# Squared-ReLU attention and a capacity-routed expert layer on one core: one z piece per go, goes of four in the whole first group, and the three engines' order fixed from the first step

## The chip, the core and the metric

The kernel runs on one core of one Trainium2 chip. The core's engines work side by side, each through its own list of instructions in order: TensorE (PE in the rows; its weight loads are PEld), VectorE (DVE), ScalarE (ACT), GpSimd (POOL) and SyncE (SP, which here issues the plain DMAs). An engine that reaches an instruction whose operands are not ready stands still, and so does everything behind it in its list. The metric is the device time of one execution in microseconds.

## The reference, cut to what matters

```python
# u, v: (8, 2496, 256); z: (8, 2496, 64)
scores = (1 / 2496) * np.matmul(z, z.transpose(0, 2, 1))
attn = np.maximum(scores, 0.0) ** 2
out = u * np.matmul(attn, v)                     # (8, 2496, 256)
x = out.reshape(19968, 256)                      # then the expert layer
logits = x @ w_gate                              # 8 experts, 2496 tokens each at most
# tokens go to experts greedily, in falling order of logit; y = relu(x @ w1[e]) @ w2[e]
```

Everything is float32. The change is in the attention part alone.

## The kernel before

**Numbers as two parts.** A float32 value is kept as a high part that TensorE takes directly and a low part, value minus high part. A product is made of three passes: high by high, high by low, low by high. So z is held as `zh` and `zl`, v as `vh` and `vl`, and the squared scores as `hi` and `lo`.

**Steps.** Attention runs over 800 steps (b, g, kt): 8 batches, 5 groups of 512 queries (the last of 448), 20 key tiles of 128 (the last of 64). A batch is 100 steps, a group 20. Loop index n drives everything; `LA = 4`, `GO = 10`, `KT = 20`.
- `scores` makes a "go" of steps at once on TensorE: for each pair of key tiles three passes of two 64-row matmuls (line 863) into two of the six PSUM buffers `sc`. A go is named here by the n at which it stands: go n makes the scores of steps n+4 and on. Before the change the goes have 4, 4, 4 and 2 steps, then ten each.
- `rectify` empties an `sc` buffer into an `r` tile, on ScalarE (line 875); the second of each go of ten is done on VectorE (line 873).
- `square` (ScalarE, line 879), `split_hi` (ScalarE line 884, or for three in ten VectorE line 886) and `split_lo` (VectorE, line 895) follow for step n+4, one step per n.
- `av(n)` multiplies with v on TensorE: six matmuls of 512 columns per step (lines 908, 910, 911) into `acc`.
- `split_v` makes `vh` on ScalarE (844) and `vl` on VectorE (845); in the first batch one key tile per step.
- After a group, `take_acc`, `turn_back`, `post_mul` and the gate logits (line 959, VectorE, 32 per group spread over later steps) finish its rows.

**z pieces.** The transposed z of a batch, tiles `zh` and `zl`, is made in five pieces, one for each four key tiles. `load_z` brings a piece in by DMA (`zin`, two buffers). `z_turn` transposes it on TensorE (two matmuls, line 807) into an `sc` buffer. For batches 1 to 7 `z_whole` copies that to `zsh` (ScalarE, line 814) and subtracts to `zsl` (VectorE, line 815), one buffer each, and eight DMAs (line 821) put the two tiles into `zh` and `zl`. For the first batch `z_parts` writes the pieces into place by engine (lines 830, 831) and `swap_z` copies the other halves by DMA. In `at(m, z_turn, b, g)` the number m is the step: before the change batch b, with first step n0 = 100 b, turns its pieces at n0-59, n0-55, n0-49, n0-46 and n0-43, which is two in go n0-60 and three in go n0-50.

**What sets the order.** From n = 10 to the last steps TensorE, ScalarE and VectorE run in the order in which the code is written (`tc.manual_schedule`, lines 1070 to 1072). Ahead of that, and on SP throughout, a scheduler that works with estimated costs places the instructions.

Of the kernel before, what the change touches and what calls it, by code (L numbers as in the profile page):

```python
# [21 lines left out]
def tile_attention_then_moe(ctx, tc, u, v, z, w_gate, w1, w2, out):  # L22
# [40 lines left out]
    nc.vector.tensor_scalar(first["at0"], at0_f, 4096.0, -32768.0, op0=OP.mult, op1=OP.add)  # L63

    attention(tc, u, v, z, w_gate, xd, identf, made, first, 1.0 / S)
    moe(tc, xd, first, jp, identf, w1, w2, out, B, S, consts)

# [638 lines left out]
def attention(tc, u, v, z, w_gate, xd, identf, made, first, scale):  # L706
    nc = tc.nc
    B, S, D = u.shape
    DQ = z.shape[-1]
    lg, m = first["lg"], first["m"]  # L710
# [3 lines left out]
    KT = NT + 1  # L714
    DH = D // 128
    NQ = KT // 4
    J = B * NT + B // 2
    JP = lg.shape[1]
    LA = 4
    RING = KT + 2  # L720
    SCB = 6
    GO = KT // 2
    with ExitStack() as ctx:
# [99 lines left out]
        def z_parts(b, g):  # L823
            c = slice(512 * g, 512 * g + 512)
            p = ZT.pop((b, g))
            zh, zl = [t[b][:, c].rearrange("p (i s q) -> p i s q", s=2, q=128) for t in (ZH, ZL)]
            src = p[:, :256].rearrange("p (i q) -> p i q", q=128)
            for s in range(2):
                r = slice(DQ * s, DQ * s + DQ)
                nc.scalar.activation(zh[r, :, s], src[r], AF.Copy)  # L830
                nc.vector.tensor_sub(zl[r, :, s], src[r], zh[r, :, s].bitcast(F32))

        def swap_z(b, c):
# [16 lines left out]
        def width(g):  # L850
            return min(512, S - 512 * g)

        def scores(lo, hi):
            for n in range(lo, hi, 2):
                b, g, kt = seq[n]
                w = width(g)
                q = slice(g * 512, g * 512 + w)
                pair = [ps.tile([128, 512], F32, name="sc", bufs=SCB)[:, :w] for _ in range(2)]
                for key, query in ((ZH, ZH), (ZH, ZL), (ZL, ZH)):
                    for s in range(2):  # L860
                        r = slice(DQ * s, DQ * s + DQ)
                        k = (kt + s) * 128
                        nc.tensor.matmul(pair[s], key[b][r, k:k + 128], query[b][r, q],  # L863
                                         start=key is ZH and query is ZH, stop=key is ZL)
                for s in range(2):
                    SC[n + s] = pair[s]
                    rectify(n + s, n + s == lo + 1 and hi - lo == GO)

        def rectify(n, aside):
            p = SC.pop(n)  # L870
            r = wk.tile([128, 512], F32, name="r", bufs=GO + 3)[:, :p.shape[1]]
            if aside:
                nc.vector.tensor_scalar(r, p, 0.0, scale, op0=OP.max, op1=OP.mult)
            else:
                recent["r"] = nc.scalar.activation(r, p, AF.Relu, scale=scale)  # L875
            R[n] = r

        def square(n):
            nc.scalar.activation(R[n], R[n], AF.Square)  # L879

        def split_hi(n):
            h = wk.tile([128, 512], F32R, name="hi", bufs=LA + 1)[:, :width(seq[n][1])]
            if (n - LA) % GO not in (0, 4, 8):
                nc.scalar.activation(h, R[n], AF.Copy)  # L884
            else:
                nc.vector.tensor_copy(h, R[n])
            HI[n] = h

        def split_lo(n):
            a, h = R.pop(n), HI[n]  # L890
            if seq[n][2] == NT:
                nc.vector.tensor_sub(h[TL:], a[TL:], h[TL:].bitcast(F32))
                return
            l = wk.tile([128, 512], F32R, name="lo", bufs=LA + 1)[:, :width(seq[n][1])]
            recent["l"] = nc.vector.tensor_sub(l, a, h.bitcast(F32))  # L895
            LO[n] = l

        def av(n):
            b, g, kt = seq[n]
            if kt == 0:  # L900
                ACC[b, g] = [ps.tile([128, 512], F32, name=f"acc{d}", bufs=1) for d in range(2)]
            last = kt == NT
            h, l = HI.pop(n), LO.pop(n, None)
            for d in range(2):
                o = ACC[b, g][d][:, :width(g)]
                c = slice(d * 128, (d + 1) * 128)
                vh, vl = VH[b, kt][:, c], VL[b, kt][:, c]
                nc.tensor.matmul(o, vh, h, start=(kt == 0), stop=False)  # L908
                if not last:
                    nc.tensor.matmul(o, vh, l, start=False, stop=False)  # L910
                nc.tensor.matmul(o, vl, h, start=False, stop=last)  # L911
# [84 lines left out]
        def at(n, f, *a):  # L996
            todo.setdefault(n, []).append((f, a))

        def logits_at(m0):
            if m0 + KT < B * NQ * KT:  # L1000
                mid, end = {NQ - 3: (18, 14), NQ - 2: (10, 14)}.get(m0 // KT % NQ - 1, (14, 14))
                return [m0 + GO] * mid + [m0 + KT] * end + [m0 + KT + 4 + i for i in range(4 * E - mid - end)]
            return [m0 + GO] * 16 + [m0 + GO + 1 + i // 3 for i in range(16)]
# [7 lines left out]
        for b in range(B):  # L1011
            for g in range(NQ):
                n0 = (b * NQ + g) * KT
                m0 = n0 + KT
                t = m0 + (0 if m0 == B * NQ * KT else 2)
                for d in range(2):
                    at(m0 - 1, take_acc, b, g, d)
                at(t, turn_back, b, g)
                for d in range(2):
                    at(t + 1, post_mul, b, g, d)  # L1020
                for e, n in enumerate(logits_at(m0) if m0 < B * NQ * KT else ()):
                    first_in.setdefault(n, []).append((post_logits, (b, g, e // E, e % E)))
                if b or g:
                    at(n0 - 3, load_u, b, g)
            n0 = b * NQ * KT
            if b == B - 1:
                at(B * NQ * KT + 2, last_logits, b, NQ - 1)
                at(B * NQ * KT + 3, settle, b * NT + 4 * (NQ - 1), (b + 1) * NT)
                at(B * NQ * KT + 3, settle, B * NT, J)
            if b:  # L1030
                for g in range(NQ):
                    m = n0 - 3 * KT + (4 * g + 1 if 4 * g + 2 < GO else KT - 3 * (NQ - g))
                    at(m - 5, load_z, b, g)
                    at(m, z_turn, b, g)
                    at(m + 1, z_whole, b, g)
                    at(n0 - KT + 4 * g - 8, load_v, b, g)
                for kt in range(KT):
                    at(n0 - KT + kt, split_v, b, kt)
            else:
                for kt in range(KT):  # L1040
                    at(kt - 4, split_v, 0, kt)
                for g in range(1, NQ):
                    t = min(4 * g - LA, GO) - 1
                    at(t, z_turn, 0, g)
                    at(t, z_parts, 0, g)
                    at(t + 1, swap_z, 0, slice(512 * g, 512 * g + 512))
                    if g >= 3:
                        at(4 * g - 13, load_z, 0, g)
                        at(4 * g - 11, load_v, 0, g)
# [11 lines left out]
        at(13, load_gate)  # L1061
        at(18, gate_rows)
        N = len(seq)
        begins = [0, LA, 2 * LA, 3 * LA] + list(range(LA + GO, N, GO))
        goes = {lo - LA: (lo, hi) for lo, hi in zip(begins, begins[1:] + [N])}
        fixed = ExitStack()
        for n in range(-LA, N + 4 * E):
            if n == 2:
                early.close()
            if n == GO:  # L1070
                fixed.enter_context(tc.manual_schedule(
                    engines={mybir.EngineType.PE, mybir.EngineType.Activation, mybir.EngineType.DVE}))
            if n == N - 4:
                fixed.close()
            if n in goes:
                scores(*goes[n])
            for f, a in first_in.pop(n, []):
                f(*a)
            m = n + LA
            if 0 <= m < N:  # L1080
                square(m)
                split_hi(m)
                split_lo(m)
            for k in sorted(k for k in todo if k < n):
                for f, a in todo.pop(k):
                    f(*a)
            if 0 <= n < N:
                av(n)
            for f, a in todo.pop(n, []):
                f(*a)  # L1090
# [25 lines left out]
```

## Time and profile before

| what | us |
|---|---|
| median of 3 runs | 2606.8 (2606.2 to 2617.64) |
| the profiled execution: its time | 2609.21 |
| its span, first to last instruction | 2607.4 |
| PE busy / DVE busy / ACT busy | 2522.9 / 2016.1 / 1543.1 |
| PE busy from 120.1 to 161.3 (41.2 long) | 37.3 |
| PE busy from 1393.3 to 1428.9 (35.6 long) | 35.6 |

The span is the profiler's view of one execution; 1.8 us lie around it. A busy time counts what an engine spent in instructions, so 2607.4 less 2522.9 is the time in which TensorE had nothing running. The last two rows are the same kind of stretch, three goes and a bit in the second batch (with z pieces for the next one) and two goes in the last batch (which has no next one).

### The profile page before, as it was taken

What the parts mean: (1) busy time and instruction counts of PE and PEld (TensorE: products, weight loads), DVE (VectorE), ACT (ScalarE), POOL (GpSimd) and SP (SyncE); (2) the same over time, 40 slices, a digit from 0 to 9 for tenths busy, and PEclk for the clock granted to TensorE, in tenths of its full rate; (3) what the DMA queues carried; (4) which work ended last, traced back from release to release, by engine and by line L of the source; (5) the groups of instructions that cost most, each with busy time, mean ns of one, the idle gap of its engine ahead of it and who ended that gap; (6) DMA issues with size and microseconds to landing.
All of it is one profiled execution on the core that took longest, in us unless ns stands there. A gap on an engine that the chain in (4) does not pass through costs nothing.

```text
span 2607.4 us, 44969 instructions
## 1 busy us (share of the span) xinstructions
PE 2522.9 (97%) x16328; PEld 2137.9 (82%) x16328; DVE 2016.1 (77%) x6105; ACT 1543.1 (59%) x2901; POOL 358.7 (14%) x507
## 2 busy tenths in 40 slices
PE   8999999999999999999999989999999999999998
PEld 5778787788788788787878768888989898989997
DVE  5788788888798898888888878869686968696322
ACT  7878788787788788787888412323333333333332
POOL 2000000000000000000000003233333333334321
PEclk9999999999999999999999989999999999999999
DMA  4121221210221221212100011112121212121110
GB/s 138 55 70 51 72 66 48 78 63 32 83 72 33 67 72 58 75 57 62 51 32 25 16 42 46 62 46 74 40 73 40 74 40 72 41 90 56 47 42 24
DMA packets 93599, 148.82 MB, mean 57 GB/s; under 512 B 16192, under 2 KB 61632, under 8 KB 93376
## 3 DMA queue, kind: packets, MB, share of 16 engines
q1 hardware_dynamic: 78272, 105.03, 13.0%
q0 software_dynamic: 15104, 40.91, 5.0%
q8 instruction: 128, 2.10, 0.3%
q14 instruction: 95, 0.78, 0.1%
HBM read 85.60 MB, written 40.89 MB: 49 GB/s over the span
## 4 chain that ended last, share of the span: by engine, by line
PE 82%; DVE 10%; ACT 3%; DMA 2%; issue 1%; SPq 1%; POOL 0%; POOLq 0%; DVEq 0%; ACTq 0%
PE acc L908 13%; PE acc L911 12%; PE acc L910 12%; PE sc L863 10%; PE y L602 5%; PE hp L571 5%; PE y L604 5%; PE y L603 5%; PE hp L572 5%; PE hp L573 5%; PE srch L243 2%; PE sc L931 1%; PE xp L555 1%; ACT r L879 1%; DMA zl<-zsl 1%
## 5 line engine op out<-in xcount | busy, mean ns | idle before, releaser
L908 PE MATMUL acc<-hi,vh 128*128 128x512 f32 (+1 forms) x1600 | 633.6, 396 | 4.2 <-ACT vh L844 3.7
L911 PE MATMUL acc<-hi,vl 128*128 128x512 f32 (+1 forms) x1600 | 617.7, 386 | 0.0
L895 DVE TENSOR_TENSOR lo<-r,hi 128x512 fp32r<-128x512 f32 (+1 forms) x760 | 504.2, 677 | 115.2 <-ACT hi L884 105.6
L910 PE MATMUL acc<-lo,vh 128*128 128x512 f32 (+1 forms) x1520 | 587.4, 387 | 0.4 <-DVE lo L895 0.2
L590 ACT ACTIVATE hh<-hp 128x512 fp32r<-128x512 f32 (+1 forms) x320 | 187.6, 586 | 548.4 <-PE hp L573 470.3
L879 ACT ACTIVATE r<-r 128x512 f32<-128x512 f32 (+1 forms) x800 | 474.1, 621 | 0.2
L959 DVE SCALAR_TENSOR_TENSOR lt<-xs,wgb 128x256 bf16<-128x256 f32 x1248 | 447.8, 421 | 0.5
L884 ACT ACTIVATE hi<-r 128x512 fp32r<-128x512 f32 (+1 forms) x560 | 348.3, 622 | 140.2 <-issue 83.9
L875 ACT ACTIVATE r<-sc 128x512 f32<-128x512 f32 (+1 forms) x722 | 364.2, 611 | 90.7 <-PE sc L863 84.8
L908 PEld LDWEIGHTS acc<-hi,vh 128*128 128x128 f32 x1600 | 301.6, 189 | 85.2 <-issue 28.6
L602 PE MATMUL y<-w2h,hh 128*128 128x256 f32 (+1 forms) x1280 | 366.9, 287 | 1.2 <-ACT y L629 1.2
L603 PE MATMUL y<-w2l,hh 128*128 128x256 f32 (+1 forms) x1280 | 363.0, 284 | 0.0
L911 PEld LDWEIGHTS acc<-hi,vl 128*128 128x128 f32 x1600 | 301.3, 188 | 58.0 <-issue 1.3
L910 PEld LDWEIGHTS acc<-lo,vh 128*128 128x128 f32 x1520 | 287.0, 189 | 49.8 <-DVE lo L895 1.8
L571 PE MATMUL hp<-xh,w1h 128*128 128x512 f32 (+2 forms) x646 | 262.7, 408 | 0.7 <-ACT xh L564 0.7
L572 PE MATMUL hp<-xl,w1h 128*128 128x512 f32 (+2 forms) x646 | 251.2, 389 | 0.0
L602 PEld LDWEIGHTS y<-w2h,hh 128*128 128x128 f32 (+1 forms) x1280 | 241.2, 188 | 11.8 <-ACT y L629 1.6
L573 PE MATMUL hp<-xh,w1l 128*128 128x512 f32 (+2 forms) x646 | 249.8, 387 | 0.0
L603 PEld LDWEIGHTS y<-w2l,hh 128*128 128x128 f32 (+1 forms) x1280 | 241.0, 188 | 8.8
L635 POOL DMA_INDIRECT out_dram<-y,idx x160 | 176.7, 1105 | 385.3 <-ACT y L629 337.5
L863 PE MATMUL sc<-zh 64*128 64x512 f32 (+1 forms) x800 | 192.7, 424 | 26.6 <-DVE zsl L815 11.8
L496 POOL DMA_INDIRECT xg<-xd,idx x160 | 162.9, 1018 | 389.3 <-PE xp L555 133.1
(1159 smaller groups left out, 3721.8 us busy)
## 6 DMA issues: line engine op xcount, KB each, us to landing
vr<-in_v_dram SPq DMA_DIRECT2D x32, 512.0 KB, 3.7
ur<-in_u_dram SPq DMA_DIRECT2D x32, 512.0 KB, 4.3
xd<-xs SPq DMA_DIRECT2D x32, 512.0 KB, 2.9
wr<-in_moe_w_dram SPq DMA_DIRECT2D x32, 512.0 KB, 5.3
zh<-zsh SPq DMA_DIRECT2D x140, 64.0 KB, 2.1
zl<-zsl SPq DMA_DIRECT2D x140, 64.0 KB, 2.0
zin<-in_z_dram SPq DMA_DIRECT2D x31, 128.0 KB, 2.2
vr<-in_v_dram SPq DMA_DIRECT2D x8, 384.0 KB, 3.3
```

The lines of the kernel that those rows point to most:

```text
L571: nc.tensor.matmul(p[:, c], wh, xh, start=(d == 0), stop=False)
L572: nc.tensor.matmul(p[:, c], wh, xl, start=False, stop=False)
L573: nc.tensor.matmul(p[:, c], wl, xh, start=False, stop=(d == DH - 1))
L602: nc.tensor.matmul(o, h[:, c], wh, start=first, stop=False, skip_group_check=True)
L603: nc.tensor.matmul(o, h[:, c], wl, start=False, stop=False, skip_group_check=True)
L863: nc.tensor.matmul(pair[s], key[b][r, k:k + 128], query[b][r, q], start=key is ZH and query is ZH, stop=key is ZL)
L879: nc.scalar.activation(R[n], R[n], AF.Square)
L895: recent["l"] = nc.vector.tensor_sub(l, a, h.bitcast(F32))
L908: nc.tensor.matmul(o, vh, h, start=(kt == 0), stop=False)
L910: nc.tensor.matmul(o, vh, l, start=False, stop=False)
L911: nc.tensor.matmul(o, vl, h, start=False, stop=last)
L959: nc.vector.scalar_tensor_tensor(t[r], XS[b, g][r, i], 1.0, WG["rows"][r, e], op0=OP.mult, op1=OP.mult, accum_out=lg[r, j, e:e + 1])
```

## The change

- Batches 1 to 7 turn one z piece per go, five steps after its start: m = n0 + 10 (g - 8) + 5, so n0-75, -65, -55, -45, -35; `load_z` stands nine steps ahead instead of five.
- The first group is made in goes of four to its end: 4, 4, 4, 4, 4, 4, then ten each. From step 24 on goes begin where they did.
- In a go of any length (so in the last one of six too) the second rectification is on VectorE.
- In the first group all high parts are made on VectorE.
- In the first batch the turn of piece g, its parts and its swap stand at steps 4g-7, 4g-6 and 4g-5, and both ScalarE parts stand ahead of both VectorE parts.
- The written order holds on the three engines from n = -4, the first step.

```diff
             for s in range(2):
                 r = slice(DQ * s, DQ * s + DQ)
                 nc.scalar.activation(zh[r, :, s], src[r], AF.Copy)
+            for s in range(2):
+                r = slice(DQ * s, DQ * s + DQ)
                 nc.vector.tensor_sub(zl[r, :, s], src[r], zh[r, :, s].bitcast(F32))
...
-                    rectify(n + s, n + s == lo + 1 and hi - lo == GO)
+                    rectify(n + s, n + s == lo + 1)
...
-            if (n - LA) % GO not in (0, 4, 8):
+            if n >= KT and (n - LA) % GO not in (0, 4, 8):
                 nc.scalar.activation(h, R[n], AF.Copy)
             else:
                 nc.vector.tensor_copy(h, R[n])
...
-                    m = n0 - 3 * KT + (4 * g + 1 if 4 * g + 2 < GO else KT - 3 * (NQ - g))
-                    at(m - 5, load_z, b, g)
+                    m = n0 + GO * (g - 2 * NQ + 2) + 5
+                    at(m - 9, load_z, b, g)
                     at(m, z_turn, b, g)
                     at(m + 1, z_whole, b, g)
...
-                    t = min(4 * g - LA, GO) - 1
+                    t = 4 * g - LA - 3
                     at(t, z_turn, 0, g)
-                    at(t, z_parts, 0, g)
-                    at(t + 1, swap_z, 0, slice(512 * g, 512 * g + 512))
+                    at(t + 1, z_parts, 0, g)
+                    at(t + 2, swap_z, 0, slice(512 * g, 512 * g + 512))
...
-        begins = [0, LA, 2 * LA, 3 * LA] + list(range(LA + GO, N, GO))
+        begins = list(range(0, KT + LA, LA)) + list(range(KT + LA, N, GO))
...
-            if n == GO:
+            if n == -LA:
                 fixed.enter_context(tc.manual_schedule(
                     engines={mybir.EngineType.PE, mybir.EngineType.Activation, mybir.EngineType.DVE}))
```

ScalarE in the first batch, go n = 50, before: the pieces of batch 1 pass through `zsh` (`at0` closes the group; `hi` and `r` belong to steps 55 to 63).

```order
L884 ACTIVATE hi_1433<-r_1339 128x512
L814 ACTIVATE zsh_1443<-sc_1429 128x256
L879 ACTIVATE r_1341<-r_1341 128x512
L884 ACTIVATE hi_1460<-r_1341 128x512
L879 ACTIVATE r_1351<-r_1351 128x512
L879 ACTIVATE r_1353<-r_1353 128x512
L884 ACTIVATE hi_1485<-r_1353 128x512
L814 ACTIVATE zsh_1494<-sc_1481 128x256
L879 ACTIVATE r_1363<-r_1363 128x512
L884 ACTIVATE hi_1507<-r_1363 128x512
L814 ACTIVATE zsh_1544<-sc_1530 128x256
L919 ACTIVATE at0_1565<-acc0_1152 128x512
```

The same engine and go in the changed kernel, where line numbers are two higher from there on: one piece is left in this go.

```order
L886 ACTIVATE hi_1478<-r_1368 128x512
L881 ACTIVATE r_1378<-r_1378 128x512
L886 ACTIVATE hi_1491<-r_1378 128x512
L814 ACTIVATE zsh_1501<-sc_1487 128x256
L881 ACTIVATE r_1380<-r_1380 128x512
L886 ACTIVATE hi_1518<-r_1380 128x512
L881 ACTIVATE r_1390<-r_1390 128x512
L881 ACTIVATE r_1392<-r_1392 128x512
L886 ACTIVATE hi_1542<-r_1392 128x512
L921 ACTIVATE at0_1550<-acc0_1188 128x512
```

The other two pieces of the three stand in goes n = 40 and n = 60 now.

VectorE at the start of the program, before: steps 0 to 3 and the first batch's z piece 1 (`zl_126<-sc_194`), as the scheduler placed them.

```order
L895 TENSOR_TENSOR lo_161<-r_142,hi_159 128x512
L845 TENSOR_TENSOR vl_164<-vr_113,vh_163 128x256
L895 TENSOR_TENSOR lo_170<-r_144,hi_168 128x512
L845 TENSOR_TENSOR vl_173<-vr_113,vh_172 128x256
L886 CAST hi_177<-r_154 128x512
L895 TENSOR_TENSOR lo_179<-r_154,hi_177 128x512
L845 TENSOR_TENSOR vl_182<-vr_113,vh_181 128x256
L895 TENSOR_TENSOR lo_188<-r_156,hi_186 128x512
L845 TENSOR_TENSOR vl_191<-vr_113,vh_190 128x256
L831 TENSOR_TENSOR zl_126<-sc_194,zh_125 64x2x128 x2
```

The same place in the changed kernel: a rectification (line 875) comes first, every step has its `hi` here, and the z piece stands between the third and the fourth step.

```order
L875 TENSOR_SCALAR r_146<-sc_137 128x512
L888 CAST hi_161<-r_144 128x512
L897 TENSOR_TENSOR lo_163<-r_144,hi_161 128x512
L847 TENSOR_TENSOR vl_166<-vr_113,vh_165 128x256
L888 CAST hi_170<-r_146 128x512
L897 TENSOR_TENSOR lo_172<-r_146,hi_170 128x512
L847 TENSOR_TENSOR vl_175<-vr_113,vh_174 128x256
L888 CAST hi_182<-r_156 128x512
L897 TENSOR_TENSOR lo_184<-r_156,hi_182 128x512
L847 TENSOR_TENSOR vl_187<-vr_113,vh_186 128x256
L833 TENSOR_TENSOR zl_126<-sc_178,zh_125 64x2x128 x2
L888 CAST hi_195<-r_158 128x512
```

TensorE where the second go of scores is made, before: the scheduler took `av` of steps 0 to 2 first, and put matmuls of step 2 and 3 (`acc`) in between the scores (`sc`).

```order
L910 MATMUL acc1_233<-lo_179,vh_181 128x512
L863 MATMUL sc_203<-zh_125 128x512
L863 MATMUL sc_203<-zl_126,zh_125 128x512
L911 MATMUL acc0_232<-hi_177,vl_182 128x512
L911 MATMUL acc1_233<-hi_177,vl_182 128x512
L908 MATMUL acc0_232<-hi_186,vh_190 128x512
L910 MATMUL acc0_232<-lo_188,vh_190 128x512
L863 MATMUL sc_203<-zh_125,zl_126 128x512
L863 MATMUL sc_204<-zh_125 128x512
L863 MATMUL sc_204<-zl_126,zh_125 128x512
L863 MATMUL sc_215<-zh_125 128x512
```

In the changed kernel the second go (`sc_209` to `sc_222`) stands right behind the turn of z piece 1 (`sc_178`), whole, and ahead of the first `acc`.

```order
L807 MATMUL sc_178<-identf_63,zin_115 128x128 x2
L865 MATMUL sc_209<-zh_125 128x512
L865 MATMUL sc_210<-zh_125 128x512
L865 MATMUL sc_209<-zl_126,zh_125 128x512
L865 MATMUL sc_210<-zl_126,zh_125 128x512
L865 MATMUL sc_209<-zh_125,zl_126 128x512
L865 MATMUL sc_210<-zh_125,zl_126 128x512
L865 MATMUL sc_221<-zh_125 128x512
L865 MATMUL sc_222<-zh_125 128x512
L910 MATMUL acc0_238<-hi_161,vh_165 128x512
```

Of each pair of scores the third pass (`zh_125,zl_126`) reads the low part of the new keys, `zl`.

## Rows read from the trace of the kernel before

**Rows 1.** The page: span, and busy time of each engine with its share.
```profile
span 2607.4 us, 44969 instructions
PE 2522.9 (97%) x16328; PEld 2137.9 (82%) x16328; DVE 2016.1 (77%) x6105; ACT 1543.1 (59%) x2901; POOL 358.7 (14%) x507
```

**Rows 2.** Waits of TensorE from 80 to 1450 us: engine, line <- what ended the wait: us in total, times, longest.
```profile
PE sc L863 <- DVE zsl L815: 11.8, 7, 2.3
PE sc L807 <- DMA zin<-in_z_dram: 6.9, 7, 1.8
PE sc L863 <- DVE r L873: 5.8, 7, 0.8
PE sc L863 <- ACT r L875: 5.1, 7, 0.9
```

**Rows 3.** TensorE in order of time, the first matmul of a go: start, duration. 84.05 and 1357.81 are the same go (n = 30 and n = 730) seven batches apart; 101.13 and 161.32 are goes n = 40 and n = 70, and 1374.91 and 1428.93 goes n = 740 and n = 770 of the last batch.
```profile
84.05 0.50 PE L863 MATMUL sc<-zh 64*128 64x512 f32 x2
101.13 0.50 PE L863 MATMUL sc<-zh 64*128 64x512 f32 x2
161.32 0.51 PE L863 MATMUL sc<-zh 64*128 64x512 f32 x2
1357.81 0.50 PE L863 MATMUL sc<-zh 64*128 64x512 f32 x2
1374.91 0.50 PE L863 MATMUL sc<-zh 64*128 64x512 f32 x2
1428.93 0.50 PE L863 MATMUL sc<-zh 64*128 64x512 f32 x2
```

**Rows 4.** SP's queue in order of time: start, us, the copies of z pieces (four of `zh`, then four of `zl` each). The first copies of pieces 2, 3 and 4 of batch 1, and the last of piece 4.
```profile
129.01 2.62 SPq L821 DMA_DIRECT2D zh<-zsh  x4
...
135.01 2.54 SPq L821 DMA_DIRECT2D zh<-zsh  x4
...
141.88 2.55 SPq L821 DMA_DIRECT2D zh<-zsh  x4
144.53 2.60 SPq L821 DMA_DIRECT2D zl<-zsl  x4
```

**Rows 5.** Waits of VectorE and ScalarE for the single `zsl` and `zsh` buffers from 80 to 1450 us, in the columns of rows 2, and the time of these copies from issue to landing.
```profile
DVE zsl L815 <- DMA zl<-zsl: 41.7, 14, 4.2
ACT zsh L814 <- DMA zh<-zsh: 22.3, 11, 3.9
DMA to landing us min/median/max: 2.0/2.0/4.1
```

**Rows 6.** TensorE around the turn of piece 1 (go n = 40) in order of time: the matmul ahead, the turn (two matmuls in one row), and the second matmul behind it.
```profile
114.10 0.39 PE L911 MATMUL acc<-hi,vl 128*128 128x512 f32 x1
114.33 0.38 PE L807 MATMUL sc<-identf,zin 128*128 128x128 f32 x2
...
114.78 0.40 PE L910 MATMUL acc<-lo,vh 128*128 128x512 f32 x1
```

**Rows 7.** TensorE in the first group, in order of time; two matmuls of one row on `acc` start one behind the other. The last row is the start of go n = 20.
```profile
12.05 1.22 PE L908 MATMUL acc<-hi,vh 128*128 128x512 f32 x2 [1.58 <-ACT vh L844]
13.07 1.06 PE L910 MATMUL acc<-lo,vh 128*128 128x512 f32 x2
13.93 1.05 PE L911 MATMUL acc<-hi,vl 128*128 128x512 f32 x2
...
64.19 0.50 PE L863 MATMUL sc<-zh 64*128 64x512 f32 x2
```

**Rows 8.** A stretch of the first group: us, PE busy (instructions), PEld, DVE, ACT, POOL, granted clock, DMA share, GB/s.
```profile
40.30:50.55 10.25, 8.78 (x33) 5.40 (x33) 4.01 (x8) 7.23 (x15) 0.00 (x0) 0.50 0.34 101
```

**Rows 9.** ScalarE at the start, in order of time: two rectifications, a square, a `vh`, a square.
```profile
10.09 1.09 ACT L875 ACTIVATE r<-sc 128x512 f32<-128x512 f32 x2
...
13.21 0.64 ACT L879 ACTIVATE r<-r 128x512 f32<-128x512 f32 x1
13.73 0.43 ACT L844 ACTIVATE vh<-vr 128x256 fp32r<-128x256 f32 x1
14.04 0.64 ACT L879 ACTIVATE r<-r 128x512 f32<-128x512 f32 x1
```

**Rows 10.** VectorE at the start, in order of time: `hi`, `lo`, `vl`, the next `lo`, and half of a z piece.
```profile
14.31 0.42 DVE L886 CAST hi<-r 128x512 fp32r<-128x512 f32 x1
14.77 0.69 DVE L895 TENSOR_TENSOR lo<-r,hi 128x512 fp32r<-128x512 f32 x1
15.38 0.42 DVE L845 TENSOR_TENSOR vl<-vr,vh 128x256 fp32r<-128x256 f32 x1
15.71 0.69 DVE L895 TENSOR_TENSOR lo<-r,hi 128x512 fp32r<-128x512 f32 x1
...
16.65 0.41 DVE L831 TENSOR_TENSOR zl<-sc,zh 64x256 fp32r<-64x256 f32 x1
```

**Rows 11.** VectorE, then TensorE, around the start of go n = 20, in order of time: the two copies of the gate's rows, the go's rectification on VectorE, and the matmul that waited for it.
```profile
63.47 2.28 DVE L748 COPY wgb<-wg 128x1024 f32<-128x1024 f32 x2
...
66.99 0.68 DVE L873 TENSOR_SCALAR r<-sc 128x512 f32<-128x512 f32 x1
67.72 0.50 PE L863 MATMUL sc<-zh 64*128 64x512 f32 x1 [0.94 <-DVE r L873]
```

**Rows 12.** The chain that ended last, a piece of it in the last steps of attention.
```profile
1463.03 4.53 DVE lt L959 x27
```

## The prediction

> **What bounds the kernel now.** I read the page first: TensorE is busy for 97% of the span [rows 1], so a gain can only come from the 84.5 us in which it stands still (2607.4 less 2522.9) or from matmuls that run slowly. Second I read TensorE's waits in the steady part of attention, 80 to 1450 us [rows 2]: four kinds, each of them seven times, a single one near 1 or 2 us. Seven is the number of batches whose z is turned ahead. Third I laid the starts of TensorE's goes side by side [rows 3]. Goes 40, 50 and 60 of the first batch take 161.32 - 101.13 = 60.19 us; the same three goes of the last batch, which turns no z, take 1428.93 - 1374.91 = 54.02. The reader is to see that 6.17 us per batch hang on z pieces. The first batch stands for all: its period is within 0.1 us of the mean of seven, (1357.81 - 84.05) / 7 = 181.97 (from 84.05 to the same go a batch later the trace shows 182.04).
>
> Why three pieces in one go hurt is in SP's queue [rows 4]: the copies of pieces 2, 3 and 4 begin at 129.01, 135.01 and 141.88, and those of piece 4 end at 147.13 (144.53 + 2.60). So a piece takes 5.25 us of that queue (147.13 - 141.88), and some 2 us more until they land [rows 5]; pieces follow each other at 6.0 and 6.9 us. In the program they are turned three steps apart, which is 5 us. `zsh` and `zsl` have one buffer each, so ScalarE and VectorE stand for the copies of the piece before (22.3 and 41.7 us in all [rows 5]), with everything behind them in their lists, until TensorE runs out of free `sc` buffers: it waits for `zsl` 2.3 us at worst, then for the rectification on VectorE [rows 2].
>
> The other place is the first group. Go n = 20 begins at 64.19 and go n = 30 at 84.05 [rows 7, 3]. In it TensorE was at half clock in two stretches: the matmuls of 13.07 and 13.93 stand 0.43 us apart (two in 0.86) [rows 7] where full speed has 0.23 (114.10 to 114.33 [rows 6]), and from 40.30 to 50.55 the granted clock was 0.50 [rows 8].
>
> **Term 1, one z piece per go.** The copies of a piece take 5.25 us of queue and 2 to land; goes last 17 us and more (101.13 - 84.05 = 17.08 [rows 3]). So no piece meets the one before, and no wait is left on `zsh`, `zsl` or, with the load nine steps ahead and the tail parts of `zin` no longer queued behind a neighbour's copies, on `zin`. What stays is the turn itself: 114.10 to 114.78 is 0.68 us where two matmuls take 0.46, so a turn costs TensorE 0.22 [rows 6]. Five of them are 1.1 per batch, in 6.17 as well as afterwards. Gain: 6.17 - 1.1 = 5.07 per batch, 35.5 in seven. ScalarE and VectorE get 0.4 us of work in goes 20, 30 and 60 that had none; over the run both have idle time (77% and 59% busy [rows 1]), and in the mid-go position (step 5) piece 1 of batch 1 already stands without a wait behind it on TensorE. If that cover is missing, each new go loses up to 0.4: 3 x 7 x 0.4 = 8.4. Bounds: at most all of it, 35.5; at least half, 17.7, if the wait only moves. I take 35.
>
> **Term 2, the first group.** I walk the written order, each instruction starting when its engine is free and its operands are there.
> - Intervals: on ScalarE rectifications 0.48 apart, square to `vh` 0.52, `vh` to square 0.31 [rows 9]; on VectorE `hi` to `lo` 0.46, `lo` to `vl` 0.61, `vl` to next 0.33 [rows 10], so 1.40 a step, and 0.75 for the two halves of a z piece (0.33 + 0.42).
> - Head. As before the third and fourth rectification start at 10.09 [rows 9]; they take ScalarE to 11.05, the square ends at 11.7, then three steps on VectorE bring 15.9 and z piece 1 is complete at 16.65. The second go of scores stands ahead of all `acc` work, and its third pass needs that piece. So `acc` work that began at 12.05 [rows 7] now begins behind a pair's third pass at 16.65, four passes later (18.4). This is a loss of 6 us, paid at the outset.
> - Clock. Before, TensorE worked without a break from 12.05 and the rate rose at about 16.4, 4.4 us later. I take the same from 16.65: 21.0. By then ten passes are done at 0.43; the remaining 18 of the 28 (4 scores, 24 `acc`) take 4.1 and the turn 0.22: go 8 (n = 4) begins at 25.3.
> - Cycle. At full clock a go is 6 passes of scores, 24 of `acc` and a turn: 30 x 0.228 + 0.22 = 7.06 us of TensorE. The other chain: scores of the first pair complete 0.85 in, of the second 1.55 in, two rectifications to 2.5, square to 3.2, three steps on VectorE to 7.4, the z piece at 8.15. The next go's third pass, 0.46 behind that go's start, needs it: so goes repeat not at 7.06 but at about 7.7 to 7.8. From 25.3: 32.4 (first go undelayed), 40.2, and then the go that needs no new piece at 47.8 (n = 16); its 6 + 22 passes take 6.4, so go n = 20 begins at 54.2 instead of 64.19.
> - Go n = 20. It lasted 19.86 before. It gets the first turn (0.22), and the two gate-row copies (2.28 [rows 11]) stand in VectorE's list closer behind the fast goes: the rectification came 2.8 us into the go before (66.99) and cost a wait of 0.94 [rows 11]; I walk it to 3.8, one more us. So 21.1, and go n = 30 begins at 75.3 instead of 84.05: gain 8.7.
>
> Bounds of term 2: with TensorE never waiting for the z piece, three cycles are 0.7 shorter and the gate copies cost nothing more: 12. With the half clock lasting to 40 instead of 21, the walk ends at 83: 1.
>
> Here a rule of the Trainium skill speaks against the change: in "TensorE: Matmul & The Clock Gate", section "What's actually happening", half rate is the default state and activity releases it. By that rule a first group with short pauses in every go might not be released, which is the fourth case below. The trace agrees that work with pauses can run at half clock: in the stretch at 0.50 TensorE was busy for 8.78 us of 10.25 [rows 8].
>
> **Term 3, the tail.** The last go of six has its second rectification on VectorE now, 0.68 us [rows 11], and the chain there runs through VectorE's logits (4.53 us in one piece [rows 12]). Cost 0.5; between 0 and 0.7. The remaining moves cost nothing on the path: high parts on VectorE (`hi`, 0.46 a step) are inside the 1.40 above, and two ScalarE z parts ahead of two VectorE ones only remove an alternation.
>
> **Sum.** 35 + 8.7 - 0.5 = 43.2 us off the profiled execution's 2609.21: 2566. That execution is 2.4 above the median of the runs, 2606.8; against it 2563.6. I say 2564.
>
> **Rivals.**
> 1. The first group gains nothing (clock late, or the 6 us of the head not won back): 2606.8 - 35 + 0.5 = 2572. For it: the head starts worse. Against: before, the scheduler's order lost the clock between 40.30 and 50.55.
> 2. Half of the z wait stays, moved: ScalarE or VectorE meet `zsh` late in each go, or SP's queue, whose order is still the scheduler's, puts a load that waits ahead of the copies. 2606.8 - 17.7 - 8.7 + 0.5 = 2581. For it: a longest wait of 4.2 [rows 5] came from queueing. Against: 17 us between pieces and 7.3 of copies.
> 3. Slower: a turned piece holds one of six `sc` buffers until VectorE has made `zsl`; if that comes late in each of the 35 goes that now have a piece, as at the worst wait for it, 2.3, with the 0.8 for the rectification behind it [rows 2], 35 x 3.1 = 108 are paid instead of 35.5: 2606.8 + 73 - 8.7 = 2671. It decides from (35.5 + 8.7) / 35 = 1.26 us per go on. Against: the piece is turned at step 5, so five steps, 8 us, lie ahead of the next scores.
> 4. Half clock through the whole first group: a cycle is then 30 x 0.43 + 0.3 = 13.2 instead of 7.8; three of them and the slower go n = 16 add some 28 to the walk, go n = 30 at 103, 19 later than before: 2606.8 - 35 + 19 = 2591. For it: a pause of 0.7 in each go. Against: pauses as long stand in steady stretches at full clock (0.94 at 67.72 [rows 11]).
>
> **Chances and range.** Forecast 0.76 (own range 2556 to 2571: term 1 from 30 to 35.5, term 2 from 6 to 12 and the spread of the runs), rival 1: 0.08, rival 2: 0.09, rival 3: 0.04, rival 4: 0.03. The range 2553 to 2582 takes in the first two rivals. A change of 0.5%, 13 us, is about what the measurement tells from none. Faster by more (under 2594): 0.76 + 0.08 + 0.09 and 0.02 of rival 4, 0.95; within: 0.01 each of rivals 3 and 4; slower: the other 0.03 of rival 3.
>
> **What would show it.** Goes 40 to 60 together 54.7 us instead of 60.2, goes 20 and 30 each 0.2 longer, and no TensorE wait ended by `zsl` or `zin`; no wait of ScalarE or VectorE for the copies. Copies of one piece per 17 us on SP. The first `acc` matmul near 18.4, go n = 20 near 54, go n = 30 near 75; VectorE waiting for the first square of each go of four. The first `av` earlier than 16 or the clock at 0.50 past 30 would make term 2 wrong; a wait for `sc` in goes 20 to 70 would make term 1 wrong.

## The result, and the profile after

The changed kernel takes 2565.97 us (median of 4 runs, 2565.08 to 2566.29); beside it the kernel before took 2606.9. The ratio is 0.9833, with a 95% interval of 0.9807 to 0.9858: 41 us less, where 43 were forecast. The profiled execution has a span of 2564.1, 43.3 less than [rows 1]. TensorE's busy time fell by 17.1 us and the time in which it stood by 26.2, from 84.5 to 58.3. Part of the fall in busy time lies ahead of go n = 30 (counted from 4 us on, 71.2 before and 65.0 after) and 1.1 in the first of the seven batch periods (177.4 and 176.4); the rest was not taken apart.

The page of the changed kernel, the span and the busy times:
```profile
span 2564.1 us, 44934 instructions
PE 2505.8 (98%) x16328; PEld 2133.8 (83%) x16328; DVE 2024.3 (79%) x6125; ACT 1531.1 (60%) x2881; POOL 364.2 (14%) x507
```

The only wait of TensorE left from 80 to 1420 us, against the four of [rows 2], and below it the longest wait of any engine there, against [rows 5] (waiting instruction <- what ended the wait: us in total, times, longest):
```profile
PE sc L865 <- ACT r L877: 5.0, 7, 0.8
```
```profile
DVE lo L897 <- ACT hi L886: 112.0, 216, 1.2
```
`zsl`, `zin` and the rectification on VectorE are gone from TensorE's list, and no engine waits for a copy. What ScalarE and VectorE wait for is ordinary work: new scores, and high parts.

The copies on SP in the first batch (start, duration), against [rows 4]:
```profile
106.90 2.63 SPq L821 DMA_DIRECT2D zh<-zsh  x4
...
124.70 2.64 SPq L821 DMA_DIRECT2D zh<-zsh  x4
```
One piece per 18 us, where 6.0 and 6.9 lay between the three of go n = 50 before.

TensorE in order of time, the first matmul of the goes n = 30, 40, 70 and 730, against [rows 3]:
```profile
75.45 0.50 PE L865 MATMUL sc<-zh 64*128 64x512 f32 x2
92.81 0.51 PE L865 MATMUL sc<-zh 64*128 64x512 f32 x2
147.59 0.50 PE L865 MATMUL sc<-zh 64*128 64x512 f32 x2
1314.65 0.50 PE L865 MATMUL sc<-zh 64*128 64x512 f32 x2
```
Goes 40 to 60 take 147.59 - 92.81 = 54.78 us instead of 60.19, and a batch (1314.65 - 75.45) / 7 = 177.03 instead of 181.97.

The first group on TensorE, against [rows 7]: the first scores of n = -4 and of n = 0, the first `acc`, and the first scores of n = 4, 8, 12, 16 and 20 (in brackets the idle time ahead and what ended it). The matmul ahead of go n = 4 and the one behind its first two are there too, for the distance at a change between `acc` and scores:
```profile
5.87 0.80 PE L865 MATMUL sc<-zh 64*128 64x512 f32 x2 [0.69 <-ACT zh L804]
13.00 0.68 PE L865 MATMUL sc<-zh 64*128 64x512 f32 x1 [3.28 <-ACT zh L830]
17.89 0.79 PE L910 MATMUL acc<-hi,vh 128*128 128x512 f32 x1
24.50 0.39 PE L913 MATMUL acc<-hi,vl 128*128 128x512 f32 x1
24.81 0.50 PE L865 MATMUL sc<-zh 64*128 64x512 f32 x2
25.15 0.40 PE L865 MATMUL sc<-zl,zh 64*128 64x512 f32 x2
32.31 0.50 PE L865 MATMUL sc<-zh 64*128 64x512 f32 x2
40.35 0.50 PE L865 MATMUL sc<-zh 64*128 64x512 f32 x2
47.83 0.51 PE L865 MATMUL sc<-zh 64*128 64x512 f32 x2
54.65 0.50 PE L865 MATMUL sc<-zh 64*128 64x512 f32 x2
```
Two stretches of it, against [rows 8] (columns as there):
```profile
13.10:20.00 6.90, 6.09 (x17) 3.75 (x18) 5.57 (x13) 4.20 (x10) 4.48 (x42) 0.51 0.78 273
24.50:53.60 29.10, 29.10 (x144) 21.54 (x143) 23.65 (x49) 21.07 (x46) 2.93 (x29) 1.00 0.40 110
```
From 13 to 20 the clock is 0.51; from 24.50 on TensorE has no pause for 29 us and the clock is 1.00, with matmuls 0.23 apart. The stretch of 10 us at 0.50 that stood in the old group is gone. A busy TensorE can still lose a little: in these 29 us its weight loads waited three times for the first batch's z pieces, 0.5 us in go n = 8 and 0.2 in go n = 12:
```profile
PEld sc L865 <- DVE zl L833: 0.7, 3, 0.3
```

The time went as follows: 34.6 us in seven batch periods (7 x 4.94), 8.6 before go n = 30 (84.05 less 75.45), and 0.1 in the rest: 43.3.

### The profile page after: what moved, and what is told of

It reads as the page before. It is cut to its first block, busy times and chain, and to the rows that moved or that the text cites. A ratio compares the mean times of both kernels' runs of the same rounds, so it can differ in the third digit from the quotient of the medians.

```text
span 2564.1 us, 44934 instructions
## 1 busy us (share of the span) xinstructions
PE 2505.8 (98%) x16328; PEld 2133.8 (83%) x16328; DVE 2024.3 (79%) x6125; ACT 1531.1 (60%) x2881; POOL 364.2 (14%) x507
## 4 chain that ended last, share of the span: by engine, by line
PE 84%; DVE 9%; ACT 3%; DMA 1%; issue 1%; POOL 0%; POOLq 0%; ACTq 0%; DVEq 0%; SPq 0%
PE acc L910 13%; PE acc L913 13%; PE acc L912 12%; PE sc L865 11%; PE hp L571 5%; PE y L602 5%; PE y L604 5%; PE y L603 5%; PE hp L572 5%; PE hp L573 5%; PE srch L243 2%; PE sc L933 1%; ACT r L881 1%; PE xp L555 1%; DVE ob L443 1%
## 5 line engine op out<-in xcount | busy, mean ns | idle before, releaser
L886 ACT ACTIVATE hi<-r 128x512 fp32r<-128x512 f32 (+1 forms) x546 | 339.4, 622 | 143.0 <-issue 76.2
```

## The experiments

The first four of these kernels ran on one chip, the next four on a second and the last four on a third. A median is compared with that of the kernel before on the same chip: 2606.46, 2655.7 and 2607.38. What concerns a few us is read from the traces, from the first score to go n = 30 ("the head"). It is 77.43 in the kernel before (84.05 - 6.62, the 6.62 being the first score in its trace) and 69.58 in the changed kernel (75.45 - 5.87).

### The z pieces alone
```
-   m = n0 - 3 * KT + (4 * g + 1 if 4 * g + 2 < GO else KT - 3 * (NQ - g))
-   at(m - 5, load_z, b, g)
+   m = n0 + GO * (g - 2 * NQ + 2) + 5
+   at(m - 9, load_z, b, g)
```


> Before with the new steps of the z pieces alone (one piece per go of ten, loaded nine steps ahead); the first group stays as before. Theory (the waits were for the one staging buffer, and the first group's gain is separate): the five middle batches' period falls from 181.97 to about 177.0 us, 34.6 us less over seven batches, so 2606.9 - 34.6 = 2572.3 us, TensorE's waits for zsl and zin gone, go n=30 still at 84.05 us. Rival (the two edits need one another, or the late part is paid by the order of the first steps): less than 30 us, above 2577.

Measured: 2573.53 us, ratio 0.9874 (0.986 to 0.9889), 32.9 less than before. The starts of goes n = 30 and n = 730:
```profile
82.62 0.50 PE L863 MATMUL sc<-zh 64*128 64x512 f32 x2
1322.04 0.50 PE L863 MATMUL sc<-zh 64*128 64x512 f32 x2
```
The period is (1322.04 - 82.62) / 7 = 177.06, that of the full change, and of the four waits only that for ScalarE is left (5.4 us). Two lines of steps carry the whole of term 1, and they do it without the new first group.

### The first group alone
```
-   m = n0 + GO * (g - 2 * NQ + 2) + 5
-   at(m - 9, load_z, b, g)
+   m = n0 - 3 * KT + (4 * g + 1 if 4 * g + 2 < GO else KT - 3 * (NQ - g))
+   at(m - 5, load_z, b, g)
```


> After with the old steps of the z pieces; the first group is the new one. Theory (additive): go n=30 begins at about 75.5 us, the batch period is 181.97 us again, the time is 2606.9 - 8.6 = 2598.3 us, with the waits for zsl and zin back. Rival (the early start only moves a wait into the first batches): 2603 to 2607.

Measured: 2601.14 us, ratio 0.9987 (0.9975 to 0.9998), 5.3 less than before. The first score and go n = 30, and the wait for `zsl` that is back (that for `zin` is too, 6.8 us):
```profile
5.71 0.80 PE L865 MATMUL sc<-zh 64*128 64x512 f32 x2 [0.69 <-ACT zh L804]
75.84 0.50 PE L865 MATMUL sc<-zh 64*128 64x512 f32 x2
```
```profile
PE sc L865 <- DVE zsl L815: 11.2, 7, 2.4
```
The head lasts 70.13, so the new group works alone too; the batch period is 181.97 again (from 75.84 to 1349.60 in seven). But the gain in time is under the 8.6 expected, and the interval leaves at most 6.5; the median lies between what was expected (2598.3) and what the rival said (2603 to 2607). The old head explains part of it: it is not the same in each execution. The run above with the old group has 82.62 - 6.50 = 76.12, the next one 75.84, and the profile before 77.43. From the mean of these, 76.5, to the new heads (69.4 to 70.3 in five runs with it) are 6 to 7 us. The 8.6 hold for the two profiled executions.

### Two buffers instead of other steps
```
-   t = io.tile([128, 4, 2, DQ], F32, name="ztwo", bufs=1)
+   t = wk.tile([128, 4, D], F32, name="ztwo", tag="xs", bufs=2)
+   t = t.rearrange("p i d -> p (i d)")[:, :8 * DQ].rearrange("p (i s d) -> p i s d", s=2, d=DQ)
...
-   h, l = [io.tile([128, 256], F32R, name=name, bufs=1) for name in ("zsh", "zsl")]
+   h, l = [io.tile([128, 256], F32R, name=name, bufs=2) for name in ("zsh", "zsl")]
```


> Before with its old steps of the z pieces, but two buffers each for zsh and zsl instead of one (room is made by putting the twice-loaded first z piece into a buffer that the gate uses later). Theory (the wait is the reuse of the one buffer behind eight copies of the piece before, 5.25 us of queue and 2 us of landing against 5.15 us between pieces): the waits of DVE for zsl and ACT for zsh fall from 41.7 and 22.3 us to under 5, the TensorE waits for zsl (11.8 us) go, those for zin may stay (up to 7 us), the time falls by 20 to 35 us, to 2572 to 2587. Rival (the SP queue or the sc buffer that a piece holds is what binds, so spacing is needed and more buffers don't help): less than 8 us, above 2599.

Measured: 2579.78 us, ratio 0.9898 (0.9883 to 0.9912), 26.7 less than before. The longest TensorE wait from 80 to 1420 but that for ScalarE, and the two goes:
```profile
PE sc L808 <- DMA zin<-in_z_dram: 6.7, 7, 1.3
```
```profile
81.39 0.50 PE L864 MATMUL sc<-zh 64*128 64x512 f32 x2
1330.18 0.50 PE L864 MATMUL sc<-zh 64*128 64x512 f32 x2
```
The period is 178.40: of the 4.94 us that the new steps give per batch, a second buffer alone gives 3.57, with the pieces as close as before. No wait of VectorE or ScalarE for the copies is left. So the single `zsh` and `zsl` are shown to be the cause of most of it. The wait for `zin` stays, 0.96 per batch, and is most of the other 1.37. Here SP's queue has its part: for the turn that waits 0.94 us in the first batch, the last part of the load begins at 131.64, behind copies that end at 131.59. Whether the earlier load or the wider spacing removes this wait in the changed kernel isn't told apart.

### Two pieces per go
```
-   m = n0 + GO * (g - 2 * NQ + 2) + 5
+   m = n0 - 69 + 5 * g
```


> After with the z pieces five steps apart (two per go of ten, some 8.6 us apart) instead of ten. Theory (a piece keeps its buffer 5.25 us in the queue and 2 us until the last copy has landed, 7.3 us, less than 8.6): no wait comes back, the time stays within 2 us of after, 2564 to 2568. Rival (one piece per go of ten is what is needed, for the queue or the loads): some of the wait of 11.8 + 6.9 us comes back, 2572 to 2585.

Measured: 2566.14 us, ratio 0.9842 (0.983 to 0.9855), the changed kernel's time. The period, from goes n = 30 and 730, is (1317.68 - 77.09) / 7 = 177.23; the one wait of TensorE is again for ScalarE (5.4 us):
```profile
77.09 0.50 PE L865 MATMUL sc<-zh 64*128 64x512 f32 x2
1317.68 0.50 PE L865 MATMUL sc<-zh 64*128 64x512 f32 x2
```
So TensorE needs no whole go per piece. But five steps are 8.6 us only in the mean: in the first batch `zsl` is made at 86.32, 93.20, 103.94, 111.77 and 122.94, so two pieces in a pair are 6.9 and 7.8 us apart, with 11 between pairs. VectorE again waits for the copies, as 5.25 us of queue and 2 of landing let expect:
```profile
DVE zsl L815 <- DMA zl<-zsl: 4.4, 8, 0.9
```
These short waits, against 41.7 us before [rows 5], don't reach TensorE. How close pieces may stand before they do is not shown.

### The turn at the end of the go
```
-   m = n0 + GO * (g - 2 * NQ + 2) + 5
+   m = n0 + GO * (g - 2 * NQ + 2) + 8
```


> After with each z piece turned three steps later (at the ninth step of a go instead of the sixth), so that its sc buffer is free only shortly before the next go's third pair of scores wants it. Theory (zsl is done some 2 us after the transposes, and the third pair begins 2.75 us after the go): 0 to 0.3 us per go, 2566 to 2576, with short TensorE waits for zsl. Rival (a piece that holds an sc buffer at the go's end costs 1.26 us or more in each of some 33 goes, the point from which the change would have lost): 2608 or more.

Measured: 2609.82 us against 2655.7, ratio 0.9828 (0.9807 to 0.9849); the period is 177.04. In time around go n = 60, left out what has no part in it:
```profile
127.46 0.38 PE L807 MATMUL sc<-identf,zin 128*128 128x128 f32 x2
...
128.71 0.50 PE L865 MATMUL sc<-zh 64*128 64x512 f32 x2
...
129.58 0.41 DVE L815 TENSOR_TENSOR zsl<-sc,zsh 128x256 fp32r<-128x256 f32 x1
...
130.19 0.42 PE L865 MATMUL sc<-zh 64*128 64x512 f32 x2
```
Here `zsl` is made only after the next go has begun, and is done at 129.99. That go's sixth score, which gets the piece's buffer, belongs to the third pair, and this begins at 130.19, 1.48 us into the go (the expectation had put it at 2.75). So 0.2 us are to spare, and in seven batches no wait of TensorE for `zsl` is listed, only the one for ScalarE (5.6 us). Rival 3 needed 1.26 us per go; with the turn three steps later it still gets none.

### The first square earlier
```
+   early_square = set()
...
     for s in range(2):
         SC[n + s] = pair[s]
         rectify(n + s, n + s == lo + 1)
+    if n == lo and hi - lo < GO:
+        square(lo)
+        early_square.add(lo)
...
-    square(m)
+    if m not in early_square:
+        square(m)
```


> After with the first square of each go of four issued ahead of the go's third and fourth rectification on ScalarE. Theory (the goes of four last 7.5 to 8.0 us because two rectifications stand ahead of the first square, and TensorE's own work in them is 7.06 us): the goes from n=4 to n=16 last 7.1 to 7.4 us, go n=20 begins 2 to 4 us earlier, the time falls by 2 to 4 us to 2562 to 2564. Rival (the later rectifications hold the sc buffers longer or make the later squares late, so the wait only moves): within 1 us of after.

Measured: 2608.84 us, ratio 0.982 (0.9798 to 0.9841). The first score, go n = 20 and go n = 30:
```profile
6.64 0.80 PE L866 MATMUL sc<-zh 64*128 64x512 f32 x2 [0.69 <-ACT zh L805]
54.20 0.50 PE L866 MATMUL sc<-zh 64*128 64x512 f32 x2
74.75 0.50 PE L866 MATMUL sc<-zh 64*128 64x512 f32 x2
```
To go n = 20 it is 47.56 where the changed kernel has 48.78: 1.2 us, less than expected, and 0.5 of it lie ahead of go n = 4. The head is 68.11, 1.5 us shorter. The goes from n = 4 on last 7.50, 7.53, 7.25 and 6.80, against 7.50, 8.04, 7.48 and 6.82. With the chain shortened two of the four hardly move; n = 8 loses 0.5 and n = 12 loses 0.2, which are the waits for the z piece in the changed kernel, and none of them is left. So it isn't the chain that makes these goes longer than 7.06 but, those 0.7 us aside, TensorE's own work: 7.25 without a turn, 7.50 with one.

### The gate rows later
```
-   todo, first_in = {}, {}
+   todo, first_in = {}, {20: [(gate_rows, ())]}
...
-   at(18, gate_rows)
```


> After with the two copies of the gate rows moved on VectorE from ahead of go n=20's first rectification to behind its scores. Theory (the 2.31 us of copies make that rectification 3.46 us late and TensorE waits 1.62 us for it): the wait goes and go n=30 begins 1.5 to 2 us earlier, 2564 us. Rival (the copies then delay the first splits of go n=20, and the wait only changes its name): within 0.5 us of after, or 1 us slower.

Measured: 2610.06 us, ratio 0.9824 (0.9803 to 0.9845). Goes n = 20 and n = 30, and of the changed kernel the wait that this removes:
```profile
55.18 0.50 PE L865 MATMUL sc<-zh 64*128 64x512 f32 x2
73.90 0.50 PE L865 MATMUL sc<-zh 64*128 64x512 f32 x2
```
```profile
58.86 0.49 PE L865 MATMUL sc<-zh 64*128 64x512 f32 x1 [1.62 <-DVE r L875]
```
Go n = 20 lasts 18.72 where the changed kernel has 20.80, and the head is 67.24 (from 6.66), 2.3 us shorter. The wait is gone, and no other wait of TensorE has come in that go.

### Both


> After with both: the first square of each go of four ahead of the third rectification, and the gate rows copied behind go n=20's scores. Theory (two separate waits of the first group): the gains add, 3.5 to 6 us, 2560 to 2562.5. Rival (one shadows the other): no more than the better one of the two.

Measured: 2609.01 us, ratio 0.9821 (0.98 to 0.9842). The edits are those of the last two kernels together. The head is 66.07 (6.38 to 72.45), 3.5 us shorter than in the changed kernel and near the sum of 1.5 and 2.3. By its trace this is the better kernel; the times can't show 3.5 us (0.13%) with intervals of 0.2%.

### The order of the first steps left to the scheduler
```
-   if n == -LA:
+   if n == GO:
        fixed.enter_context(tc.manual_schedule(
```


> After, but with the order of the three engines fixed only from step 10 on, as before; the goes of four, the high parts on VectorE and the late z pieces stay. Measured from the first score to go n=30: after 69.6 us, before 77.4. Theory (the order is most of the gain: the scheduler draws the scores of later goes and the splits together and lets TensorE fall to half clock again): 73 us or more, with a stretch at 0.50 behind 20 us. Rival (goes and splits are the gain, whoever orders them): 71 us or less.

Measured: 2559.83 us, ratio 0.9812 (0.9793 to 0.9831). The theory fell. The first score, go n = 20, the gate rows' wait in that go, go n = 30, and a stretch behind the wait (us, then busy time of PE, PEld, DVE, ACT and POOL, clock, DMA share, GB/s):
```profile
6.53 0.80 PE L865 MATMUL sc<-zh 64*128 64x512 f32 x2 [0.69 <-ACT zh L804]
52.05 0.50 PE L865 MATMUL sc<-zh 64*128 64x512 f32 x2
56.29 0.50 PE L865 MATMUL sc<-zh 64*128 64x512 f32 x1 [1.65 <-DVE r L875]
74.41 0.50 PE L865 MATMUL sc<-zh 64*128 64x512 f32 x2
```
```profile
57.00:60.40 3.40, 3.40 (x14) 2.23 (x11) 0.60 (x2) 3.19 (x6) 0.00 (x0) 0.52 0.00 0
```
Go n = 20 comes 45.52 us behind the first score, 3.3 earlier than with the fixed order: the scheduler puts the first `acc` work ahead of go n = 0's scores, as the kernel before did. About 1.5 of it are lost again in go n = 20, where half clock follows the wait. The head is 67.88. So fixing the order from the very first step is no part of the gain; by these two executions it costs 3.3 us up to go n = 20 and 1.7 in the whole head (69.58 against 67.88), of which a part may be the earlier rise of the rate (0.23 us between matmuls from 16.3 on instead of 20.0). The median is 7 us below that of the changed kernel on the same chip (below), but in the profiled executions go n = 730 comes only 0.4 us sooner and the spans are equal (2563.0 and 2562.9). The profiled one is the slowest of four here and the fastest of four there, so the traces don't show what separates the medians; the intervals overlap, and the 7 us stay unexplained.

### The high parts shared as before
```
-   if n >= KT and (n - LA) % GO not in (0, 4, 8):
+   if (n - LA) % GO not in (0, 4, 8):
        nc.scalar.activation(h, R[n], AF.Copy)
```


> After, but with seven of ten high parts on ScalarE in the first group too, as before. In the goes of four TensorE's own work is 7.5 us; ScalarE is busy 5.7 us of it and VectorE 5.7 to 6.8. Theory (ScalarE gets 0.6 us for each of three high parts, 7.5 of 7.5 us, and each step then goes to and fro between two engines): the goes from n=4 to n=16 last 8 to 9 us each, first score to go n=30 72 to 75 us. Rival (both engines have room, the split of work doesn't matter): within 1 us of after's 69.6.

Measured: 2565.43 us, ratio 0.9836 (0.9818 to 0.9854). The head is 69.59 (6.12 to 75.71), that of the changed kernel, and so is the way to go n = 20 (48.79): the rival holds. Where high parts are made doesn't matter here, in goes that TensorE fills.

### The old lengths of the first goes
```
-   t = 4 * g - LA - 3
+   t = min(4 * g - LA, GO) - 1
    at(t, z_turn, 0, g)
-   at(t + 1, z_parts, 0, g)
-   at(t + 2, swap_z, 0, slice(512 * g, 512 * g + 512))
+   at(t, z_parts, 0, g)
+   at(t + 1, swap_z, 0, slice(512 * g, 512 * g + 512))
...
-   begins = list(range(0, KT + LA, LA)) + list(range(KT + LA, N, GO))
+   begins = [0, LA, 2 * LA, 3 * LA] + list(range(LA + GO, N, GO))
```


> After, but with the old lengths of the first goes (4, 4, 4, 2 and then ten) and the old steps of the z pieces in the first group; the fixed order and the high parts on VectorE stay. Theory (a go of ten at n=10 brings ten rectifications in a row, behind which the squares stand, so TensorE waits some 3 us there or its clock falls): first score to go n=30 72 to 76 us. Rival (the order alone is the gain): within 1 us of after's 69.6.

Measured: 2569.35 us, ratio 0.9851 (0.9832 to 0.9869). The first score and go n = 30:
```profile
5.70 0.80 PE L865 MATMUL sc<-zh 64*128 64x512 f32 x2 [0.69 <-ACT zh L804]
78.75 0.50 PE L865 MATMUL sc<-zh 64*128 64x512 f32 x2
```
The head is 73.05, 3.5 longer, in the range that the theory gave; but the waits of 3 us for rectifications that it named aren't there. What has come are waits for the first batch's z pieces, whose old steps the edit brings back too. From 24 to 60 us, where the changed kernel has the 0.7 us for `zl` alone:
```profile
PEld sc L865 <- ACT zh L830: 2.0, 5, 0.7
...
PE sc L865 <- ACT zh L830: 0.9, 2, 0.5
```
Ahead of go n = 4, where 2.0 of the 3.5 us lie, TensorE waits 4.1 us instead of 3.3 for the first piece's `zh` and 1.4 instead of 0.8 for its `zl`, and full speed comes 1.5 us later. So the 3.5 us belong to the goes of four and the z steps of the first batch together, and the waits that the trace lists speak for the z steps; the goes of four with the old z steps, or the other way round, were not run.

### The changed kernel once more


> After itself, as the yardstick of the three others on the same chip. First score to go n=30 69.6 us within 1 us, the ratio to before 0.983 within 0.003. If the half clock of the first group were a matter of chance rather than of order, it would come out several us longer here.

Measured: 2567.0 us, ratio 0.9843 (0.9824 to 0.9862). The head is 69.38 (6.47 to 75.85), within 0.2 of the first profile.

## Why the prediction was right

**Term 1** (35 forecast, 34.6 measured) was right in size and in cause. Two buffers alone bring most of it back with the old steps, and the z steps alone give the whole period. With pieces five steps apart VectorE waits a little for the copies and TensorE doesn't. The turn was taken at 0.22, and a go with one is 0.28 longer (75.45 to 92.81 is 17.36, where go n = 30 took 17.08 without one [rows 3]). That the five turns stay was right. The cover for the moved work of ScalarE and VectorE is there: goes 20 and 30 have no new wait of TensorE behind a z piece, and of the 8.4 us that a lack of cover could have cost nothing is seen.

**Term 2** (8.7 forecast, 8.6 between the two profiles) was right in its sum, with parts that don't hold and that offset each other.
- The walk set starts of 25.3, 32.4, 40.2, 47.8, 54.2 and 75.3; the trace has 24.81, 32.31, 40.35, 47.83, 54.65 and 75.45. But the first score came 0.75 us earlier than in the trace that the walk began from, by a start that the change doesn't touch; so from the first score the walk was 0.9 too short (68.7 to 69.58).
- The step that failed is the cycle. TensorE's work in a go of four was counted as 30 passes and a turn, 7.06; it is 7.50, because at each change between `acc` and scores two starts lie 0.31 to 0.34 apart and not 0.228 (24.50 to 24.81 to 25.15, and again from scores to `acc`). The chain over the z piece, walked to 8.15, was to be late by some 0.7 in the goes that need a new piece; it is late by 0.5 in n = 8 and 0.2 in n = 12.
- Go n = 20 lasted 20.80 (21.1 forecast): the gate rows do make the rectification late, as the run with the gate rows later shows, and the wait is 1.62 rather than 1.94.
- The first `acc` (18.4, measured 17.89) and the rate (21.0, measured 20.0) were close, but the time of the rate's rise is partly chance. So is the length of the old head, 75.8 to 77.4 in three profiles, and the gain in a mean run is nearer 7 than 8.6. That the sum came out at 8.6 is in part luck: 0.75 of it is the earlier first score.

**Term 3** was taken at a loss of 0.5. From go n = 730 to the end it is 1249.5 after (2564.1 - 1314.65) and 1249.6 before: nothing. The rectification that moved to VectorE shows no price there.

**The rivals.** Rival 1 is out: the first group gains, alone too. Rival 2 is out: no wait for the copies is left on any engine. Rival 3 found no price even when the piece is turned three steps later. Rival 4 is out by the stretch at 1.00 with TensorE busy for 29.10 of 29.10. The rule of the Trainium skill that stood behind it, that half rate is the default and activity releases it ("TensorE: Matmul & The Clock Gate", section "What's actually happening"), isn't contradicted. What the prediction made of it, that pauses in every go might keep the clock at half, wasn't tested, since the goes fill TensorE.

What the working did not tell apart is which edit of the first group gains, and the runs do it only in part. The scheduler's order of the first steps is 3.3 us better by go n = 20, sharing the high parts changes nothing, and the goes of four and the first batch's z steps together carry 3.5. The rest of the way, from the 76.5 of the old head to the 73.05 with old goes and old z steps, is not taken apart further. The half clock near 40 us, which all three profiles of the old group show (0.50 in [rows 8]; 0.50 and 0.51 from 38 to 47 with the z pieces alone and with two buffers), is absent there (1.00 from 38 to 47), and just so in the run with the new goes in the scheduler's order. So it wasn't the scheduler's order alone that lost the clock, as the prediction had it under rival 1. In the profile before, the slow matmuls are scores of goes n = 8 and n = 10, with pauses in between for z pieces of the first batch:
```profile
45.58 0.79 PE L863 MATMUL sc<-zh 64*128 64x512 f32 x1 [0.86 <-ACT zh L830]
```

## What to carry to other kernels

Where an engine waits as many times as an outer loop has turns, look for a buffer that is refilled before its reader, here eight queued copies and their landing, has let it go. Here spacing the refills past that time took the whole wait away and a second buffer most of it, and the trial of the second buffer named the cause. Before walking a chain for the time of a short cycle, count from rows of the same kind what the full engine itself does in it, its changes between kinds of work included. And take a profiled head of some tens of us as one draw: two or three executions of it belong in the estimate.

## What the runs showed of the hardware

- The rate of TensorE after the first pause rises at different times for the same instructions. In the kernel before work resumes at 12.05 and matmuls are 0.43 apart until 16.4 [rows 7]; in the run with the z pieces alone, whose first group is the same, it resumes at 11.93 and they are 0.23 apart (two in 0.46) from 12.5 on:
```profile
12.51 0.63 PE L910 MATMUL acc<-lo,vh 128*128 128x512 f32 x2
12.97 0.63 PE L911 MATMUL acc<-hi,vl 128*128 128x512 f32 x2
```
  With the new group it resumes at 13.00 and the rate is full from 20.0 on in the changed kernel; with pieces five steps apart it resumes at 13.95 and is full from 23.2.
- A granted clock of 1.00 in the first stretch of a trace is not proof of full speed. With shared high parts, the stretch from 14.60 to 20.70 shows 1.00 throughout, and its matmuls stand 0.42 to 0.43 apart, as in stretches that show half clock:
```profile
14.60:20.70 6.10, 6.10 (x17) 4.04 (x18) 4.38 (x9) 4.94 (x10) 3.79 (x40) 1.00 0.65 204
```
```profile
19.03 0.63 PE L912 MATMUL acc<-lo,vh 128*128 128x512 f32 x1
19.45 0.63 PE L913 MATMUL acc<-hi,vl 128*128 128x512 f32 x1
```
- Pauses of one length have different sequels: behind the 1.65 us at 56.29 in the run with the scheduler's order the clock fell to half for 3.4 us, behind the 1.62 us at 58.86 in the changed kernel it did not.
- The second chip ran the kernel before 49 us slower (2655.7). In the late-turn kernel go n = 730 still begins at 1314.51 there, and TensorE is busy without a pause to 1423 in both, so the difference lies behind the steady part of attention: from go n = 730 on it takes 1295.5 us (2610.0 - 1314.51) against 1249.5. The cause was not looked for; the ratios on that chip are those of the others.
